# Issuing one 2 MB weight load of a decode kernel as sixteen loads of 8 partitions

## The chip, the cores and the metric

The kernel runs on one core of one Trainium2 chip. The time is that of the device for one execution, in microseconds (us), median of several executions; most executions of one kernel agree within 0.3%. Profiles are single executions, read with times from the start of the span. "Engine" with a number (engine 5) means one of the core's 16 DMA engines; the compute engines are called by name (TensorE, VectorE). SP is the sequencer that issues nearly all loads, in one queue.

HBM is the memory that the loads read, SBUF the core's on-chip memory that they write, in 128 partitions. A port is one of the doors through which DMA engines write SBUF; which partitions lie behind one port is told where it is needed. A packet is one piece of a load, moved by one engine. A semaphore is a counter that can be waited for; a load counts it up as its parts land.

## The reference

A decode step for one token: modulation vectors from `c`, a layer norm, grouped-query attention over a cache of 65,536 positions, then a gated feed-forward block. Cut to what matters here:

```python
D, F = 1024, 3584
Hq, Hkv, Sk, Dh = 32, 4, 65536, 128
mod = silu(c) @ w_mod                                  # 12.6 MB
x = x + ga * attention(h, k_cache, v_cache, wq, wo)    # caches: 134 MB, wq and wo: 8.4 MB each
h = layernorm(x) * (1 + cb) + sb
x = x + gb * ((gelu(h @ w_gate) * (h @ w_up)) @ w_down)  # three weights of 7.3 MB each
```

All of it is bfloat16, and every byte is read once: 185.6 MB.

## The kernel before

Every large load goes into one of ten slots of 16 KB per partition, in a fixed order, from one queue. A load is issued when the slot's former contents have been used. The products with one token are matmuls with the weight as stationary operand, one per 128 x 128 block. The last thirteen loads are four of the gate projection, four of the up projection and five of the down projection:

```python
    def plan_load(src, view_fn):

        s = len(loads) % NSLOT
        nfill[s] += 1
        job = Job(view_fn(slots[s]), (fill[s], 16 * nfill[s]), s)
        job.src = src
        # ... (cut)

    def issue_ready():

        while issued[0] < len(loads):
            j = loads[issued[0]]
            if j.prev is not None:
                if j.prev.freed is None:
                    return
                SP.wait(j.prev.freed)
            sp.dma_start(j.view, j.src).then_inc(j.tok[0], 16)
            issued[0] += 1

        # ... (cut) the down projection; P = 128, UE = 4, NBF = 7
        wd_v = B_w_down.rearrange("(b p e) n -> p b e n", p=P, e=UE)
        while b + 2 < NBF:                     # three loads of 2 MB
            jb = plan_load(
                wd_v[:, b:b + 2, :, :],
                lambda t: t[:, 0:2 * UE * D].rearrange("p (b e n) -> p b e n", b=2, e=UE),
            )
            j_d.append((jb, jb.view.rearrange("p b e n -> p (b e) n"), b * UE, 2 * UE))
            b += 2
        while b < NBF:                         # two loads of 512 KB
            for e in range(0, UE, 2):
                jb = plan_load(wd_v[:, b, e:e + 2, :], flat(2, D))
                j_d.append((jb, jb.view, b * UE + e, 2))
            b += 1

        # ... (cut) the product: waits for one load after the other
            for (jb, view, k0, nk) in jobs:
                PE.wait(jb.tok)
                for kk in range(nk):
                    for j in range(nblk):
                        w = pick(view, kk, j) if pick else view[:, kk, j * P:(j + 1) * P]
                        ins = pe.matmul(bank[:, j:j + 1], w, rhs[:, k0 + kk:k0 + kk + 1], ...)
```

A 2 MB load of the down projection is 16 packets of 8 KB on each of the 16 engines. The third of them, the one that is changed, is called load 90 below (the count is from 0); 88 and 89 are the two before it, 91 and 92 the two of 512 KB behind it.

## Time and profile before

| | before |
|---|---|
| time, median | 455.26 us |
| profiled span | 454.3 us |
| DMA | 409 GB/s from HBM over the span |
| TensorE | 76% busy |

Two rows of the page cut the span into 40 slices of 11.4 us: the mean busy share of the 16 DMA engines in tenths, and what they moved.

```profile
DMA  8999999999999999999999999999999999999972
GB/s 331 429 421 421 430 420 431 418 428 423 421 424 428 423 421 431 421 423 427 423 427 423 426 421 428 423 423 428 418 428 423 426 421 427 413 419 416 419 324 108
```

The engines are busy at about 420 GB/s to the last two slices, so the kernel is bound by its loads. In the last two slices the rate falls to 324 and 108 GB/s. The table of windows shows this closer. Its columns are the stretch in us, its length, busy time and number of instructions of each compute engine, the granted clock of TensorE (as a share of full speed), the mean busy share of the DMA engines and GB/s.

```profile
core 0: us, PE busy (x) PEld busy (x) DVE busy (x) ACT busy (x) POOL busy (x), PEclk, DMA share, GB/s
425.00:430.00 5.00, 2.67 (x80) 2.58 (x78) 0.00 (x0) 0.00 (x0) 0.00 (x0) 0.50 1.02 421
...
435.00:440.00 5.00, 1.96 (x71) 1.91 (x69) 0.18 (x1) 0.00 (x0) 0.00 (x0) 0.50 0.78 323
440.00:445.00 5.00, 1.98 (x75) 1.90 (x73) 0.00 (x0) 0.00 (x0) 0.00 (x0) 0.50 0.51 206
445.00:450.00 5.00, 1.89 (x71) 1.80 (x68) 0.00 (x0) 0.00 (x0) 0.00 (x0) 0.50 0.39 159
```

From 440 us half of the DMA engines have nothing left to do (share 0.51) and the rate is half (206 GB/s). The chain of waits, in order of time, shows that the kernel waits for the other half (start, length, what):

```profile
426.01 24.83 DMA slot<-in_B_w_down_dram
...
450.89 0.60 PE kt_ps L278 x16
...
451.52 0.17 DVE t_dn L532
...
452.35 0.28 DVE y_row L538
```

The issue of the last load begins at 426 us, the load lands at 450.85, and 0.6 us of matmuls and about 3 us of small steps, the store of the result among them, end the kernel. TensorE isn't the limit:

```profile
438.54 1.85 PE L278 MATMUL kt_ps<-u_col,slot 128*128 128x1 bf16 x64 [3.04 <-DMA slot<-in_B_w_down_dram]
...
443.40 1.86 PE L278 MATMUL kt_ps<-u_col,slot 128*128 128x1 bf16 x64 [3.02 <-DMA slot<-in_B_w_down_dram]
...
448.38 2.29 PE L278 MATMUL kt_ps<-u_col,slot 128*128 128x1 bf16 x80 [3.12 <-DMA slot<-in_B_w_down_dram]
...
450.89 0.59 PE L278 MATMUL kt_ps<-u_col,slot 128*128 128x1 bf16 x16 [0.22 <-DMA slot<-in_B_w_down_dram]
```

The first three groups of matmuls wait about 3 us each for their load, the last one 0.22 us (the bracket gives the idle time before it and what ended it).

Every engine adds one to a load's semaphore when its part has landed, so the semaphore records of the trace give sixteen landings per load, in us:

```
load 0   6.50 to 7.55, all sixteen within 1.1 us
load 88  424.90 424.98 425.04 425.61 425.67 425.75 426.97 427.86 | 435.90 435.98 436.11 436.12 436.49 437.18 437.61 438.41
load 90  434.85 434.94 434.98 435.56 435.61 435.69 436.92 437.81 | 445.82 446.02 446.03 446.39 447.10 447.44 447.52 448.34
load 92  437.38 437.46 437.51 438.07 438.12 438.21 439.42 440.30 | 448.35 448.53 448.91 449.61 449.95 450.04 450.26 450.85
```

Eight engines run ahead of the other eight, by 11 us at the end. I call them the early and the late eight. The distance grows slowly over the whole kernel. The page has 61 packets of instruction fetch, about 1.07 us each by their records, whose durations repeat with period eight. If they fall on the late eight, each has 61 x 1.07 / 8 = 8.2 us of them, most of the 11.

### The profile page before, as it was taken

The page shows a single profiled execution, that of the slowest core. Times are in us where ns is not written, and L with a number is a line of the kernel's source. Part 1 is how long each engine was busy: PE and PEld are TensorE (multiplying, and loading weights), DVE is VectorE, ACT ScalarE, POOL GpSimd, SP SyncE. Part 2 cuts the span into 40 slices and gives each one's busy share as a digit, 9 for nine tenths or more (in the row PEclk, how much of TensorE's full clock was granted, in tenths as well). Part 3 has the DMA queues.
Part 4 walks back from the last instruction along what each step waited for, and adds up shares of the span by engine and source line. Part 5 has one row for each costly group of instructions (what it writes and reads, how often), then busy time and mean ns, then how long its engine had stood idle before and what let it go on. Part 6 is the DMA issues. An engine that isn't in the chain of part 4 may idle for free.

```text
span 454.3 us, 16671 instructions
## 1 busy us (share of the span) xinstructions
PE 347.1 (76%) x7849; PEld 336.6 (74%) x7849; DVE 161.7 (36%) x237; ACT 143.2 (32%) x548; POOL 3.7 (1%) x21
## 2 busy tenths in 40 slices
PE   1333478989998999989898998979998985554434
PEld 1333468979988998989898998969987974554434
DVE  1000037444645354444554444544454443110000
ACT  1000013454533335453333354533344534000000
POOL 2000000000000000000000000000000000000000
PEclk9999999785879568776868676895598775555555
DMA  8999999999999999999999999999999999999972
GB/s 331 429 421 421 430 420 431 418 428 423 421 424 428 423 421 431 421 423 427 423 427 423 426 421 428 423 423 428 418 428 423 426 421 427 413 419 416 419 324 108
DMA packets 15428, 186.67 MB, mean 411 GB/s; under 512 B 1536, under 2 KB 1536, under 8 KB 3840
## 3 DMA queue, kind: packets, MB, share of 16 engines
q1 hardware_dynamic: 15328, 185.61, 97.0%
q8 instruction: 61, 1.00, 0.9%
q14 instruction: 7, 0.06, 0.0%
q10 hardware_dynamic: 32, 0.00, 0.0%
HBM read 185.60 MB, written 0.00 MB: 409 GB/s over the span
## 4 chain that ended last, share of the span: by engine, by line
DMA 80%; PE 15%; ACT 2%; SPq 1%; DVE 1%; issue 1%
DMA slot<-in_A_v_cache_dram 59%; DMA slot<-in_A_wq_dram 9%; DMA slot<-in_B_w_up_dram 7%; PE kt_ps L350 6%; DMA slot<-in_B_w_down_dram 5%; PE b L420 4%; PE sc_ps L371 2%; PE kt_ps L278 1%; SPq L182 1%; ACT p_sb L407 1%; PE sc_ps L278 0%; ACT kt_sb L362 0%; PE b L388 0%; PE b L395 0%; DVE Rmat L480 0%
## 5 line engine op out<-in xcount | busy, mean ns | idle before, releaser
L350 PE MATMUL kt_ps<-ident,slot 128*128 128x128 bf16 x2048 | 181.8, 260 | 5.8 <-DMA slot<-in_A_k_cache_dram 3.5
L350 PEld LDWEIGHTS kt_ps<-ident,slot 128*128 128x128 bf16 x2048 | 157.1, 119 | 9.0 <-DMA slot<-in_A_k_cache_dram 3.9
L362 DVE COPY kt_sb<-kt_ps 128x2048 bf16<-128x2048 bf16 x96 | 117.6, 1225 | 106.5 <-PE kt_ps L350 105.6
L362 ACT ACTIVATE kt_sb<-kt_ps 128x2048 bf16<-128x2048 bf16 x32 | 60.1, 1877 | 229.4 <-PE kt_ps L350 229.4
L420 PE MATMUL b<-p_sb,slot 128*128 128x8 bf16 x2048 | 72.3, 168 | 25.6 <-DMA slot<-in_A_v_cache_dram 17.2
L420 PEld LDWEIGHTS b<-p_sb,slot 128*128 128x128 bf16 x2048 | 66.4, 101 | 27.3 <-DMA slot<-in_A_v_cache_dram 18.8
L407 ACT ACTIVATE p_sb<-sc_ps,mneg 128x64 bf16<-128x64 f32 x256 | 83.7, 559 | 4.8 <-DVE mneg L401 4.7
L407 ACT ACTIVATION_READ_ACCUMULATOR p_sb<-sc_ps,mneg 128x1 f32 x256 | 77.2, 362 | 0.0
L371 PE MATMUL sc_ps<-q_col,kt_sb 128*128 128x8 bf16 x2048 | 68.4, 167 | 1.6 <-issue 1.6
L371 PEld LDWEIGHTS sc_ps<-q_col,kt_sb 128*128 128x128 bf16 x2048 | 66.0, 100 | 2.2 <-issue 2.0
L278 PE MATMUL kt_ps<-h_col,slot 128*128 128x1 bf16 x448 | 16.2, 172 | 19.0 <-DMA slot<-in_B_w_up_dram 10.6
L278 PEld LDWEIGHTS kt_ps<-h_col,slot 128*128 128x128 bf16 x448 | 15.6, 118 | 19.7 <-DMA slot<-in_B_w_up_dram 10.9
L390 DVE TENSOR_REDUCE mg<-b 8x1 f32<-8x128 f32 x32 | 8.9, 279 | 41.9 <-PE b L388 41.9
L278 PE MATMUL sc_ps<-s_col,slot 128*128 128x1 bf16 x384 | 11.5, 165 | 15.7 <-DMA slot<-in_w_mod_dram 15.7
L384 DVE TENSOR_REDUCE m_col<-sc_ps 128x8 f32<-128x512 f32 x32 | 21.8, 681 | 4.3 <-PE sc_ps L371 4.3
L278 PEld LDWEIGHTS sc_ps<-s_col,slot 128*128 128x128 bf16 x384 | 11.0, 105 | 16.3 <-DMA slot<-in_w_mod_dram 16.3
L278 PE MATMUL sc_ps<-h_col,slot 128*128 128x1 bf16 x256 | 7.4, 165 | 12.8 <-DMA slot<-in_A_wq_dram 12.8
L278 PEld LDWEIGHTS sc_ps<-h_col,slot 128*128 128x128 bf16 x256 | 7.1, 104 | 13.2 <-DMA slot<-in_A_wq_dram 9.5
L395 PE MATMUL b<-negi,mg 8*128 8x8 f32 x64 | 15.8, 318 | 0.4 <-DVE mg L390 0.4
L395 PEld LDWEIGHTS b<-negi,mg 8*128 8x128 f32 x64 | 12.8, 249 | 2.5 <-DVE mg L390 0.6
L278 PE MATMUL kt_ps<-u_col,slot 128*128 128x1 bf16 x224 | 6.6, 165 | 9.4 <-DMA slot<-in_B_w_down_dram 9.4
L278 PEld LDWEIGHTS kt_ps<-u_col,slot 128*128 128x128 bf16 x224 | 6.3, 104 | 9.7 <-DMA slot<-in_B_w_down_dram 6.6
(71 smaller groups left out, 56.4 us busy)
## 6 DMA issues: line engine op xcount, KB each, us to landing
slot<-in_A_k_cache_dram SPq DMA_DIRECT2D x32, 2048.0 KB, 40.6
slot<-in_A_v_cache_dram SPq DMA_DIRECT2D x32, 2048.0 KB, 44.6
slot<-in_w_mod_dram SPq DMA_DIRECT2D x8, 1536.0 KB, 18.4
slot<-in_A_wq_dram SPq DMA_DIRECT2D x4, 2048.0 KB, 38.3
slot<-in_A_wo_dram SPq DMA_DIRECT2D x4, 2048.0 KB, 43.3
slot<-in_B_w_gate_dram SPq DMA_DIRECT2D x4, 1792.0 KB, 39.4
slot<-in_B_w_up_dram SPq DMA_DIRECT2D x4, 1792.0 KB, 31.2
slot<-in_B_w_down_dram SPq DMA_DIRECT2D x3, 2048.0 KB, 32.2
```

Source lines behind the costliest of these rows:

```text
L182: sp.dma_start(j.view, j.src).then_inc(j.tok[0], 16)
L278: ins = pe.matmul(bank[:, j:j + 1], w, rhs[:, k0 + kk:k0 + kk + 1], start=first, stop=True, skip_group_check=True,)
L350: ins = pe.transpose(kt_ps[:, half * 2048 + t * P:half * 2048 + (t + 1) * P], j_k[i].view[:, b * TB + t, :], ident[:, :],)
L362: ev[(i, b)] = E_.done(act.activation(dst, src, ACT.Copy) if E_ is AC else dve.tensor_copy(dst, src))
L371: ins = pe.matmul(sc_ps[:, base + n * REP:base + (n + 1) * REP], kt_sb[:, i % 2, n, :], q_col[:, g * REP:(g + 1) * REP], start=True, stop= ...
L384: mx[i] = DVE.done(dve.tensor_reduce(m_col[:, i % 2, :].unsqueeze(2), sc_view(i), AX.X, ALU.max))
L390: mx[i] = DVE.done(dve.tensor_reduce(mg8[:, i % 2:i % 2 + 1], b6[0:REP, 32:32 + P], AX.X, ALU.max))
L395: pe.matmul(b6[:, 256:256 + REP], mg8[:, i % 2:i % 2 + 1].to_broadcast([REP, P]), negi[:, :], start=True, stop=True,)
L407: act.activation(p_sb[:, i % 3, :, h], scv[:, h, :], ACT.Exp, bias=mneg[:, i, h:h + 1], scale=scale, accum_out=z_all[:, i, h:h + 1],)
L420: ins = pe.matmul(b7[:, i * REP:(i + 1) * REP], j_v[i].view[:, n, :], p_sb[:, i % 3, n, :], start=(n == 0), stop=(n == CH - 1),)
```

## The change

The intent is to even this out: load 90 is taken from all sixteen engines and given to the eight lowest alone. A load of 8 partitions has only eight shares, and the Trainium skill ("DMA: Bandwidth & Descriptors", section "Why a DMA increments its semaphore by 16 and not by 1") says that such a load runs on the lowest-numbered eight.

```diff
-    def plan_load(src, view_fn):
+    def plan_load(src, view_fn, parts=P):
+
         s = len(loads) % NSLOT
-        nfill[s] += 1
+        nfill[s] += P // parts
         job = Job(view_fn(slots[s]), (fill[s], 16 * nfill[s]), s)
         job.src = src
+        job.parts = parts
@@ issue_ready
-            sp.dma_start(j.view, j.src).then_inc(j.tok[0], 16)
+            n = j.parts
+            for a in range(0, P, n):
+                sp.dma_start(j.view[a:a + n], j.src[a:a + n]).then_inc(j.tok[0], 16)
             issued[0] += 1
@@ the 2 MB loads of the down projection
                 lambda t: t[:, 0:2 * UE * D].rearrange("p (b e n) -> p b e n", b=2, e=UE),
+                8 if b + 4 >= NBF else P,
             )
```

## The prediction

> **What bounds the kernel now.** DMA. The page's rows show the DMA engines 90% busy or more until the last two slices; the chain that ended last is 80% DMA. From 434 us that changes: the window table has DMA share 0.99 at 408 GB/s (434 to 436), then 0.51 at 206 GB/s (440 to 445) and 0.49 at 202 (445 to 448). Half of the engines have finished. The trace's semaphore records show it per load: the third down-projection load lands on eight engines at 434.9 to 437.8 us and on the other eight at 445.8 to 448.3. The last load ends at 440.3 and 450.9. The distance grows from 0.4 us at the first load to 11 us. The late eight also run the 61 instruction fetches (about 1.07 us each by the packet records, rotating with period eight). The two 8-row loads at the start, which run on the lowest eight engines, give packets that follow on engines without fetches. So the late half is engines 8 to 15.
>
> **What the change does.** In the 8 KB packets of the down projection an engine needs 0.312 us each, with 16 or with 8 engines working. The 2 MB load is 16 such packets per engine, 5.0 us. The change takes 5.0 us from each late engine and gives 5.0 us to each early one. If nothing else happened, both halves would end near 445.5: 5 us saved (estimate 450).
>
> **Cost.** The Trainium skill ("SBUF — State Buffer", Door 1: The DMA port swizzle) gives 27.6 GB/s measured for partitions 0 to 3 (one port) and 104 for 0 to 15 (four). Here an engine moves 8 KB in 0.312 us, 26 GB/s, about one port's rate. A load of 128 partitions gives each engine its own port. A load of 8 partitions reaches two, so four engines share one. If the eight engines march through the sixteen loads in step, a packet takes up to four times 0.312 us, and the 2 MB take up to 39 us in place of 9.7. They aren't quite in step: their landings of the load before spread over 3 us, and one engine spends 0.63 us on its partition. I worked out equal sharing of ports with the trace's start times in random engine order (estimate): the early half takes 17 to 25 us for the load from about 430 us and ends 2 to 10 us after 450.9, median 5. The upper 64 partitions also collide with the late engines' own ports.
>
> Issue: a queue instruction took 0.33 us unblocked; sixteen, about 5 to 8 us from 416.9 us, are ready before 430. TensorE follows each load with 0.6 to 1.9 us of matmuls and isn't the limit. All of this lies on the critical path, since the last two loads queue behind the sixteen.
>
> **Prediction.** 459.5 us, range 450 to 468 (8 in 10). Faster by over 2%: 0.01; within 2%: 0.78; slower by over 2%: 0.21.
>
> **Signs.** Down-projection packets of 8 KB on the early eight well above 0.312 us (0.5 to 1.2); late engines done near 445 to 449, early ones last; DMA share about half in the last 10 us as before, at less than 200 GB/s; the chain's down-projection wait longer than 24.8 us. Bytes unchanged; the first 415 us unchanged.
>
> **What would make it wrong.** If ports don't limit here, packets stay at 0.312 us and the time is about 450. If the eight fall fully into step, it is above 470. If the issuing queue blocks on full rings, engines 8 to 15 could run dry before the last two loads.

## The result, and the profile after

(Here and below, the time of before is that of the runs beside the kernel in question.)

| | before | after |
|---|---|---|
| time, median | 455.48 us | 470.93 us |
| range | 455.22 to 455.77 | 470.53 to 471.12 |
| ratio | 1 | 1.0338, 95% interval 1.0320 to 1.0356 |
| profiled span | 454.3 us | 469.3 us |
| HBM read | 185.60 MB | 185.60 MB |

Ratios here and below are the mean time of one kernel's fast runs over that of the other's fast runs of the same rounds, so not quite the ratio of the medians. The change costs 15.4 us, nearly four times what I forecast, and lies outside the range.

The same rows and windows of the page of the changed kernel:

```profile
DMA  8999999999999999999999999999999999999950
GB/s 342 427 420 422 429 422 429 423 420 428 427 422 423 423 427 422 427 425 423 422 428 425 423 423 427 425 423 425 426 421 423 426 424 414 417 419 344 221 147 29
```

```profile
425.00:430.00 5.00, 2.66 (x81) 2.58 (x78) 0.00 (x0) 0.00 (x0) 0.00 (x0) 0.50 1.02 413
430.00:435.00 5.00, 0.68 (x21) 0.60 (x19) 0.00 (x0) 0.00 (x0) 0.00 (x0) 0.50 0.90 216
435.00:440.00 5.00, 1.88 (x56) 1.80 (x54) 0.18 (x1) 0.00 (x0) 0.00 (x0) 0.50 0.95 221
440.00:445.00 5.00, 1.12 (x42) 1.15 (x43) 0.00 (x0) 0.00 (x0) 0.00 (x0) 0.50 0.96 221
445.00:450.00 5.00, 0.73 (x28) 0.64 (x25) 0.00 (x0) 0.00 (x0) 0.00 (x0) 0.50 0.87 174
450.00:455.00 5.00, 1.86 (x64) 1.78 (x64) 0.00 (x0) 0.00 (x0) 0.00 (x0) 0.50 0.59 175
455.00:460.00 5.00, 0.00 (x0) 0.00 (x0) 0.00 (x0) 0.00 (x0) 0.00 (x0) 0.50 0.14 51
460.00:465.00 5.00, 1.61 (x60) 1.62 (x61) 0.00 (x0) 0.00 (x0) 0.00 (x0) 0.50 0.10 43
```

Two things are new. From 430 to 445 us nearly all engines are busy (0.90 to 0.96), but at 216 to 221 GB/s, half of the former rate. From 455 us on, a tenth of the engines is busy (0.10 of 16 engines is 1.6), and these run on for 11 us.

```profile
slot<-in_B_w_down_dram SPq DMA_DIRECT2D x2, 2048.0 KB, 42.0
slot<-in_B_w_down_dram SPq DMA_DIRECT2D x16, 128.0 KB
```

The sixteen loads of 128 KB are there (the last column, the time to landing, is given only for the ordinary ones). In the chain the wait for the last load goes from 24.83 to 29.21 us, and it begins 10.6 us later:

```profile
434.85 1.80 PE kt_ps L283 x50
436.65 29.21 DMA slot<-in_B_w_down_dram
...
465.90 0.60 PE kt_ps L283 x16
```

(The page's own chain of this kernel puts 83% down to "issue". The semaphore of the sixteen loads also has one record at each issue, by the same section of the skill for the eight engines that aren't used, and I take it that the inference of releasers loses its way there. The end of the chain, above, is sound.)

TensorE waits for each load as before, only longer:

```profile
443.88 1.85 PE L283 MATMUL kt_ps<-u_col,slot 128*128 128x1 bf16 x64 [7.00 <-DMA slot<-in_B_w_down_dram]
...
452.11 1.86 PE L283 MATMUL kt_ps<-u_col,slot 128*128 128x1 bf16 x64 [6.38 <-DMA slot<-in_B_w_down_dram]
...
463.39 2.29 PE L283 MATMUL kt_ps<-u_col,slot 128*128 128x1 bf16 x80 [9.41 <-DMA slot<-in_B_w_down_dram]
```

The packet records say more. Packets of 8 KB took 0.31 us until about 429 us, in both kernels. In the changed kernel those that start between 436 and 446 us took 0.54 to 0.60 us in the median of each 2 us, and that is true of the late eight too: their parts of load 88 landed at 439.5 to 443.8 us instead of 435.9 to 438.4, those of load 89 at 448.9 to 452.1 instead of 440.9 to 443.4. After 454 us, packets of 0.31 us again, but only as many as two engines can have. In the semaphore records of load 92 fourteen landings come by 456.8 us, and two at 463.9 and 465.9.

### The profile page after: what moved, and what is told of

It is laid out like the page before. It is cut to its first block, busy times and chain, and to the rows that moved or that the text cites. A ratio compares the mean times of both kernels' runs of the same rounds, so it can differ in the third digit from the quotient of the medians.

```text
span 469.3 us, 16686 instructions
## 1 busy us (share of the span) xinstructions
PE 344.0 (73%) x7849; PEld 333.6 (71%) x7849; DVE 161.7 (34%) x237; ACT 143.1 (30%) x548; POOL 3.7 (1%) x21
## 3 DMA queue, kind: packets, MB, share of 16 engines
HBM read 185.60 MB, written 0.00 MB: 396 GB/s over the span
## 4 chain that ended last, share of the span: by engine, by line
issue 83%; DMA 14%; PE 1%; DVE 0%; POOLq 0%; ACTq 0%; POOL 0%; ACT 0%; DVEq 0%
DMA slot<-in_B_w_up_dram 7%; DMA slot<-in_B_w_down_dram 6%; DMA x_row<-in_A_x_dram 1%; PE kt_ps L283 1%; PE b L308 0%; POOLq L549 0%; ACTq L197 0%; POOL rs L318 0%; PE b L541 0%; DVE hn L320 0%; DVE y_row L543 0%; ACT th_col L266 0%; DVE ht L327 0%; DVE y_col L539 0%; DVE t_dn L537 0%
## 5 line engine op out<-in xcount | busy, mean ns | idle before, releaser
L355 PE MATMUL kt_ps<-ident,slot 128*128 128x128 bf16 x2048 | 179.5, 258 | 6.7 <-DMA slot<-in_A_k_cache_dram 3.7
L355 PEld LDWEIGHTS kt_ps<-ident,slot 128*128 128x128 bf16 x2048 | 154.8, 118 | 8.8 <-DMA slot<-in_A_k_cache_dram 4.7
L283 PE MATMUL sc_ps<-s_col,slot 128*128 128x1 bf16 x384 | 11.5, 166 | 15.9 <-DMA slot<-in_w_mod_dram 15.9
L400 PE MATMUL b<-negi,mg 8*128 8x8 f32 x64 | 15.4, 311 | 0.4 <-DVE mg L395 0.4
```

Source lines behind the costliest of these rows:

```text
L355: ins = pe.transpose(kt_ps[:, half * 2048 + t * P:half * 2048 + (t + 1) * P], j_k[i].view[:, b * TB + t, :], ident[:, :],)
L400: pe.matmul(b6[:, 256:256 + REP], mg8[:, i % 2:i % 2 + 1].to_broadcast([REP, P]), negi[:, :], start=True, stop=True,)
```

## The experiments

The first round sets four theories against each other. Theory P: several engines crowd on one write port of SBUF (the destination). Theory S: neighbouring rows of HBM are read at once (the source). Theory O: a fixed cost of sixteen small loads. Theory G, a form of P: one crowded port holds up everybody. Runs timed in rounds and their profiles were in the fast state; the three kernels with tiny loads and the one without arithmetic ran once, so their state is unknown, and their times are only told.

**Spread on both sides.** Each of the sixteen loads takes 8 partitions 4 apart instead of 8 neighbours. The Trainium skill ("DMA: Bandwidth & Descriptors", "The descriptor swizzle") has loads of all 128 partitions served so that engine 0 gets partitions 0 to 3 and 32 to 35, engine 1 the next four of each, engines 8 to 15 the upper 64 partitions in the same way, each engine writing a port of its own. With a spacing of 4, and if the eight shares go to the eight lowest engines in order, each of them writes its own port for the lower 64 partitions, and that of the engine numbered 8 higher for the upper 64.

```diff
-                sp.dma_start(j.view[a:a + n], j.src[a:a + n]).then_inc(j.tok[0], 16)
+                w = slice(a, a + n) if n == P else slice(a // 32 * 32 + a % 32 // 8, a // 32 * 32 + 32, 4)
+                sp.dma_start(j.view[w], j.src[w]).then_inc(j.tok[0], 16)
```

> Same sixteen loads of 8 partitions, but each takes partitions 4 apart (p, p+4, ..., p+28), on both sides, result still correct. Theory P (four engines crowd on one SBUF write port): the crowding of four goes away; the first eight loads run near 0.312 us per 8 KB packet, the last eight share each port with one late engine; 450 to 457 us, so within 1% of before. Theory S (HBM: eight neighbouring 8 KB rows read at once are slow): also gone here, 450 us. Theory O (a fixed cost of sixteen small loads: issue, semaphores, ring): stays near 471 us.

Measured: correct, 466.0 us, ratio 1.0232 (1.0215 to 1.0250). No theory had this: 4.8 us better than the change, but 10.6 us worse than before. The windows show why the number lies between:

```profile
430.00:435.00 5.00, 2.37 (x67) 2.20 (x64) 0.18 (x1) 0.00 (x0) 0.00 (x0) 0.50 0.89 367
435.00:440.00 5.00, 0.08 (x4) 0.11 (x5) 0.00 (x0) 0.00 (x0) 0.00 (x0) 0.50 1.03 226
440.00:445.00 5.00, 1.76 (x64) 1.68 (x63) 0.00 (x0) 0.00 (x0) 0.00 (x0) 0.50 0.87 183
...
455.00:460.00 5.00, 2.01 (x75) 2.02 (x76) 0.00 (x0) 0.00 (x0) 0.00 (x0) 0.50 0.10 43
```

While the lower 64 partitions are written (430 to 435 us) the rate is nearly full; all packets of 8 KB started before 434 us took 0.31 us. While the upper 64 are written (435 to 445 us), packets take 0.61 to 0.62 us in the median of each 2 us from 436 to 444 us, with none below 0.59 us from 438 to 444, on all the engines that are still busy: sixteen at first, fourteen (0.87 of 16) after 440 us. And again a tenth of the engines runs on from 455 us at full speed. The semaphore records settle how many: 96 of the 128 landings of the sixteen loads come by 449.8 us, 16 for each of six engines; the other 32 form two even rows of 16, one every 0.62 us, which begin after 446 us and end at 456.6 and 457.9.

**Destination and source apart.** Two kernels with a wrong result.

```diff
 # ... (cut) w as in the run before; then, first kernel
+                sp.dma_start(j.view[a:a + n], j.src[w]).then_inc(j.tok[0], 16)
 # second kernel
+                sp.dma_start(j.view[w], j.src[a:a + n]).then_inc(j.tok[0], 16)
```

> Wrong result on purpose: each of the sixteen loads reads rows 4 apart as in the run before it, but writes 8 neighbouring partitions as the change does. Theory P (destination): near 471 us, all engines' packets at 0.5 to 0.6 us. Theory S (source): near 450 us. Theory O: 471 us.

> Wrong result on purpose: each load reads 8 neighbouring rows as the change does, but writes partitions 4 apart. Theory P: 450 to 457 us, as the run with both sides spread. Theory S: near 471 us. Theory O: 471 us.

Measured: neighbours in SBUF and spread rows in HBM 470.3 us (ratio 1.0325); neighbours in HBM and spread partitions in SBUF 466.05 us (1.0232). The two numbers are those of the change and of the kernel before this one. The destination makes the difference and the source none: theory S falls.

**The lower half only.** Eight loads of 8 neighbours for partitions 0 to 63, and one ordinary load for 64 to 127.

```diff
 # ... (cut) the count of the semaphore: 9 loads instead of 16
-            for a in range(0, P, n):
+            for a in range(0, P, n) if n == P else range(0, P // 2, n):
                 sp.dma_start(j.view[a:a + n], j.src[a:a + n]).then_inc(j.tok[0], 16)
+            if n != P:
+                sp.dma_start(j.view[P // 2:], j.src[P // 2:]).then_inc(j.tok[0], 16)
```

> Only partitions 0 to 63 go as eight loads of 8 neighbouring partitions; partitions 64 to 127 as one load, which has all 16 engines. Theory P with separate ports: while the eight small loads run, the late engines write other ports and keep 0.27 to 0.31 us per packet, the early ones are slowed to 0.5 us and more; about 455 to 460 us. Theory P with a common path in front of the ports: the late engines are slowed to 0.5 us or more too, as in the changed kernel, for about half as long; 460 to 465 us.

Measured: correct, 467.8 us (ratio 1.0271), worse than either forecast. All of the late eight were slowed: their parts of load 88 landed at 440.3 to 445.9 us, against 435.9 to 438.4 before, and packets took about 0.6 us in the median from 430 to 442 us. That speaks for a common path, but the run is not clean, for two reasons that I hadn't thought of. The load of 64 partitions shares ports itself (0.53 us in the median at 448 to 450 us). And, as the next experiment shows, two of the early engines are not among the eight lowest; they came to that load at about 430 us, so the upper ports weren't free of foreign writers. The kernel without arithmetic below decides it.

**Who is early?** Behind the last load of the kernel before, sixteen tiny loads of 1 to 16 rows, each on a semaphore of its own. If a load of k rows runs on the k lowest engines, each load adds one engine to those of the load before it, and the landings name the engines.

```diff
 # ... (cut) the semaphores and their waits; this comes once the last load is issued
+            for k in range(1, 17):
+                sp.dma_start(mark[0:k, (k - 1) * 32:k * 32],
+                    A_x[0, 0, 0:k * 32].rearrange("(p c) -> p c", c=32)).then_inc(msem[k - 1], 16)
```

> The kernel before with sixteen tiny loads (1 to 16 rows of 64 bytes, each on its own semaphore) behind the last load. A load of k rows uses the k lowest engines, so the landings tell which of the engines end early (near 440 us) and which late (near 450 us). If the eight lowest are all early, as I predicted, the load of 8 rows lands eight times near 440 us. The records of the run with both sides spread say otherwise: 96 of its 128 landings come before 448.2 us and two engines start after 446 us; so I now expect six early and two late among the eight lowest. Time as before, 455 to 457 us.

Measured: 455.66 us, correct. Every load of k rows has exactly k landings (and, below 16, one record at its issue). The landing of each engine in the first tiny load that uses it:

```
engine   0      1      2      3      4      5      6      7      8      9      10     11     12     13     14     15
us     438.3  440.3  437.7  439.8  438.6  448.8  449.8  437.5  437.7  450.6  450.1  450.3  450.3  448.5  449.0  438.2
```

The early eight are 0 to 4, 7, 8 and 15. The late eight are 5, 6 and 9 to 14. So two of the eight engines that the change loads with more work are late ones. (The counts agree with the skill's rule for the choice of engines.)

The same tiny loads behind the last load of the spread kernel and of the change:

> The same sixteen tiny loads behind the last load of the kernel with both sides spread: 466 to 468 us. Two of the eight lowest engines end near 459 to 461 us, the other six near 448 to 452; the two early engines that are not among the lowest eight end near 441 us.

> The changed kernel with the sixteen tiny loads behind the last one: engines 5 and 6 end last, near 463 and 466 us, all others by 457 us; 471 to 472 us in all.

Measured: 466.3 and 470.7 us, both correct.

```
engine             0      1      2      3      4      5      6      7
spread, us       448.9  451.4  448.7  450.1  449.3  459.1  461.3  448.8
the change, us   453.3  456.8  452.0  455.3  453.0  464.0  465.7  451.8
```

In both, engines 5 and 6 end 7 to 10 us after the last of the other six, and load 92 has landed on all engines but two by 451.8 and 456.6 us. Engines 5 and 6 are what the kernel waits for at the end.

**Ports alone.** A kernel without arithmetic (a wrong result), in stages with a wait between them. Each stage issues small loads with 4 packets of 8 KB per partition, and behind them four ordinary loads, so that the engines outside the small loads work beside them.

```python
        stage("base", [], 4)
        stage("own", own(0, 4) * 3, 4)          # 8 partitions, 4 apart, in 0 to 31
        stage("other", own(1, 4) * 3, 4)        # the same in 64 to 95
        stage("adj", [slice(8 * a, 8 * a + 8) for a in range(4)] * 3, 4)
        stage("otheralone", own(1, 4) * 3, 0)   # no ordinary loads beside
        stage("adjalone", [slice(8 * a, 8 * a + 8) for a in range(4)] * 3, 0)
        stage("four", [slice(0, 4)] * 3 + [slice(32, 36)] * 3, 4)
        stage("fouralone", [slice(0, 4)] * 3 + [slice(32, 36)] * 3, 0)
        # ... (cut) one, oneown, two
```

> Wrong result on purpose: no arithmetic, only loads, in stages with a wait between them. Each stage issues small loads (4 packets of 8 KB per partition) and behind them four ordinary loads of 128 partitions, so that the engines outside the small loads work beside them. base: ordinary loads alone, 0.312 us per packet. own: 8 partitions 4 apart in 0 to 31. other: the same in 64 to 95. adj: 8 neighbours. four: 4 neighbours. one and two: one or two engines, into partitions 68 to 71. Theory P with independent ports (an engine shares only the port it writes to): other: two writers per port, 0.6 us; adj alone: up to 1.2 us for the small loads; four alone 1.2 us; one: only that engine and one other at 0.6 us, all others at 0.312. Theory G (one crowded port holds up everybody): in one, two, adj and other all sixteen engines are slowed to about 0.6 us while the small loads last. own should run at 0.312 us in both.

Measured, in windows inside the stages base, own, other, adj, otheralone, adjalone, four and fouralone, in this order (there was no compute, so the columns are length, POOL, granted clock, DMA share, GB/s):

```profile
27.00:35.00 8.00, 0.00 (x0) 1.00 1.01 426
56.00:59.00 3.00, 0.00 (x0) 1.00 1.01 421
94.00:102.00 8.00, 0.00 (x0) 1.00 1.03 213
133.00:169.00 36.00, 0.00 (x0) 1.00 1.02 142
197.00:207.00 10.00, 0.00 (x0) 1.00 0.50 208
214.00:254.00 40.00, 0.00 (x0) 1.00 0.51 67
265.00:285.00 20.00, 0.00 (x0) 1.00 1.01 105
314.00:336.00 22.00, 0.00 (x0) 1.00 0.25 27
```

Read the last two columns. Four engines that write the same four partitions move 27 GB/s together (share 0.25, last line). That agrees with the Trainium skill ("SBUF — State Buffer", "Door 1: The DMA port swizzle"), which measured 27.6 GB/s for partitions 0 to 3. With the twelve other engines working beside them on their own ports, all sixteen are busy (1.01) at 105 GB/s in all: every packet, also those of engines that share no port with anybody, took 1.25 us, four times 0.31. Eight engines in 64 to 95 run at full rate alone (208 GB/s on half of the engines); with the owners of these ports beside them, all sixteen run at half rate (213 GB/s). In that stage every one of the sixteen shares a port with another, so it doesn't set P and G apart. Small loads as such cost nothing: in the stage own the rate is that of the stage base while they last (second line). So theory O falls. Theory P in its independent form falls by the stage four, and theory G holds there: one port with four writers held up everybody. Whether ports with two writers do so too is settled by the control in the last experiment (`BASE = 64`), where only eight engines share.

Two stages didn't do what I meant. A load of one partition with four runs ran on four engines, not on one, so one was another case of four writers on one port beside the port's owner: all sixteen engines at about 1.53 us (oneown, four writers with the owner among them: 1.25 us). And in two, with two partitions per load, three engines took about 1 us per packet and the others 0.39 us: held up, but by a quarter and not by a factor of three. How strongly the rest is held up in mixed cases stays open.

**The two late engines alone.** What does the extra work of engines 5 and 6 cost when no port is shared? The spread kernel, with the upper 64 partitions' rows written to scratch in the partitions that each engine serves anyway (a wrong result).

```diff
 # ... (cut) w as in the spread kernel
+                dst = j.view[w]
+                if n != P and a >= 64:
+                    dst = kt_sb[w.start - 64:w.stop - 64:4, 0, :, :]   # ... (cut) 16 KB per partition, free by then
-                sp.dma_start(j.view[w], j.src[w]).then_inc(j.tok[0], 16)
+                sp.dma_start(dst, j.src[w]).then_inc(j.tok[0], 16)
```

> Wrong result on purpose: the sixteen loads of the kernel with both sides spread, but the last eight write scratch in partitions 0 to 31 and 32 to 63, so that each of the eight lowest engines writes only the partitions that it serves anyway. Bytes, engines and issues as there. What is left is the second load on the two late engines 5 and 6: sixteen packets, 5.0 us. They end at 448.6 and 449.6 us before, so the last landing moves from 450.5 to 454.6: 459 to 460 us, all packets at 0.312 us. If sharing ports is not what slows the packets, it stays at 466 us.

Measured: 460.0 us, ratio 1.0087 (1.0071 to 1.0102), 4.0 us over before, as forecast. From 435 to 440 us the DMA engines move 396 GB/s where the spread kernel has 226 (the line above), and packets of 8 KB took 0.31 us in the median from 430 to 450 us:

```profile
435.00:440.00 5.00, 1.85 (x64) 1.79 (x64) 0.18 (x1) 0.00 (x0) 0.00 (x0) 0.50 0.96 396
440.00:445.00 5.00, 1.87 (x64) 1.79 (x64) 0.00 (x0) 0.00 (x0) 0.00 (x0) 0.50 0.62 247
445.00:450.00 5.00, 0.00 (x0) 0.00 (x0) 0.00 (x0) 0.00 (x0) 0.00 (x0) 0.50 0.14 56
450.00:455.00 5.00, 2.46 (x86) 2.38 (x87) 0.00 (x0) 0.00 (x0) 0.00 (x0) 0.50 0.09 36
```

Load 92 lands on fourteen engines by 445.3 us, 5.6 us before the last one of before: this is the gain that the change was after. It lands on the other two at 453.4 and 454.8.

**A shift that keeps to the findings.** The engines to be loaded are the lowest four (all early), and they may write only the partitions that they serve anyway. Then the data has to lie in these partitions: the last 512 rows of `w_down` go 16 to a partition into partitions 0 to 15 and 32 to 47, by loads of 4 partitions 4 apart. Eight small matmuls with columns of the identity move the matching values of u there. The product with these rows uses partitions 0 to 47, with zeros in u for 16 to 31.

```diff
+        wl = B_w_down[(NBF - 1) * UE * P:NBF * UE * P, :].rearrange("(q t) n -> q t n", t=16)
+        pieces = [
+            (slice(BASE + 32 * h + r, BASE + 32 * h + 16, 4), slice(16 * h + r, 16 * h + 16, 4))
+            for h in range(2) for r in range(4)
+        ]                                       # BASE = 0; destination and source partitions
+        for t in (0, 8):
+            jb = plan_load(wl[:, t:t + 8, :], flat(8, D), pieces)
 # ... (cut) the rest of the loads behind these, the move of u, and the product
```

> A different way to shift work, on the kernel before: the last 512 rows of the down projection (1 MB) are laid 16 to a partition into partitions 0 to 15 and 32 to 47, by loads of 4 partitions 4 apart, which run on engines 0 to 3 alone, each into the partitions that it serves in ordinary loads too. u of these rows is moved there by eight small matmuls. The loads of the rest follow. If the time is set by which engines carry the bytes and no foreign port is written, the twelve other engines are spared 64 KB each, 2.5 us at 0.312 us per 8 KB, and engines 0 to 3 get 7.5 us more and end by 448 us: 452.5 to 454 us. If small loads on few engines slow everybody in any case, it is above 456 us.

Measured: correct, 455.67 us, ratio 1.0001 (0.9988 to 1.0013), so the time missed its forecast. The loads did what was forecast: the last landing is at 448.66 us (before: 450.85), and packets of 8 KB stay at 0.31 us in the median. But the chain now ends differently:

```profile
406.84 36.80 DMA slot<-in_B_w_down_dram
...
443.69 7.30 PE kt_ps L290 x256
...
451.01 0.18 DVE t_dn L560
```

TensorE works 7.30 us without a pause: it took the small loads' weights after those of load 89, for which it had waited until 443.64 us, and the gain of 2.2 us became a backlog of TensorE.

The control has one number changed, `BASE = 64`: the rows go to partitions 64 to 79 and 96 to 111, which engines 8 to 11 serve.

> The same kernel with one number changed: the rows go to partitions 64 to 79 and 96 to 111, which engines 8 to 11 serve in ordinary loads. Same engines, loads, bytes and matmuls. If a shared port holds up all engines, packets of all engines go to about 0.6 us for as long as the small loads last (20 us), and the time is 460 to 465 us. If ports were independent, only engines 8 to 11 would lose time, up to 10 us on three of the late engines: also up to 463 us, but with the packets of engines 5, 6, 12 to 14 at 0.312 us. If the destination doesn't matter, as own4.

Measured: correct, 467.2 us, ratio 1.0263 (1.0248 to 1.0279), 11.5 us above its twin by the medians, and 2 us above what I had given. Between 432 and 448 us the packets of 8 KB took 0.64 to 0.66 us in the median of each 2 us, and none less than 0.56 us. Here only engines 0 to 3 and the owners 8 to 11 share a port, two to each, so the others at work were held up as well. The last landing came at 460.0 us. One window of each, first the twin:

```profile
435.00:440.00 5.00, 2.30 (x79) 2.13 (x77) 0.51 (x3) 0.00 (x0) 0.00 (x0) 0.50 0.80 328
```

```profile
435.00:440.00 5.00, 2.29 (x64) 2.11 (x64) 0.53 (x3) 0.00 (x0) 0.00 (x0) 0.50 1.03 205
```

Bytes, engines, loads and the number of matmuls are the same, and the destination makes 328 or 205 GB/s.

At last, TensorE's order mended in the first of the two: the weights of the first small-load group are used between those of loads 88 and 89, when TensorE was idle.

```diff
-        matvec(acc_bank["dn"], j_d, u_col, (v_uc,), KD)
-        matvec(acc_bank["dn"], j_l, u_l, (v_l,), KD, first=False, rows=slice(BASE, BASE + 48))
+        matvec(acc_bank["dn"], j_d[:1], u_col, (v_uc,), KD)
+        matvec(acc_bank["dn"], j_l[:1], u_l, (v_l,), KD, first=False, rows=lo)
+        matvec(acc_bank["dn"], j_d[1:], u_col, (v_uc,), KD, first=False)
+        matvec(acc_bank["dn"], j_l[1:], u_l, (v_l,), KD, first=False, rows=lo)
 # ... (cut) lo = slice(BASE, BASE + 48); the last loads' product follows as before
```

> own4 with one change on TensorE only: the weights of the first small-load group, which landed at 438.3 us in own4 while TensorE sat idle from 440.6 to 443.7, are used before those of the second 2 MB load. In own4 the last byte landed at 448.7 us, 2.2 us earlier than before, and TensorE then ran 3 us behind. With 1.9 us taken off that backlog: 453.5 to 454.5 us, 0.3 to 0.5% faster than before. If it isn't TensorE that ate the gain, 455.5 us again.

Measured: correct, 454.01 us, as forecast, ratio 0.9967 (0.9954 to 0.9979). It beats both kernels, by 0.33% over the one before, clear of noise.

```profile
443.46 3.56 PE kt_ps L290 x124
...
447.35 2.07 PE kt_ps L290 x68
...
449.45 0.18 DVE t_dn L563
```

TensorE's last matmuls end 1.6 us earlier than in the run before.

## Why the prediction was wrong

**Where the time went.** By the ratios, times 455.5 us: the extra work on engines 5 and 6 costs 4.0 us (ownonly). Sharing the ports of the upper 64 partitions costs 6.6 more (spread, 10.6 in all). Writing 8 neighbours instead of 8 partitions 4 apart costs 4.8 more (the change, 15.4). The three were taken off one after the other; in another order the shares could differ.

The prediction had two terms: 450 us if ports don't limit, and 9.5 us more for crowded ports. The runs show 460.0 us without shared ports, and 10.9 us more with them. So nearly all of the miss of 11.4 us is in the first term, the engines. That the second came out near is in part luck, since the sum behind it slowed only the engines that share a port.

**Point by point.**

- "DMA", with half of the engines done 11 us early: right. The chain and the windows showed it, and shifting bytes to four early engines did move the last landing.
- "So the late half is engines 8 to 15": wrong, and this is the step that failed. The late eight are 5, 6 and 9 to 14. I inferred it from records that followed the two 8-row loads at the start: six of the eight engines with such packets had no fetch, and two seemed to have one, which I took for a mix-up in following the packets. Engines 5 and 6 are the two late ones among the eight lowest. The change therefore takes 5.0 us from six late engines only and gives 5.0 us to two of them, which end the kernel. The estimate of 5 us saved couldn't have come about even on free ports: the kernel with free ports is 4.0 us slower than before (460.0 us, not 450).
- "A load of 8 partitions reaches two [ports], so four engines share one": right in kind; four engines on one port move 27 GB/s together.
- "Equal sharing of ports", with only the sharers slowed: wrong. The whole set of engines was slowed. The signs had the late engines done near 445 to 449 us and the early ones last. In the run with the tiny loads behind the change, the late engines 9 to 14 had their parts of load 92 between 452.7 and 455.2 us (the landings that are left when those of the other ten are taken out), and two late engines, 5 and 6, came last of all.
- "The early half takes 17 to 25 us for the load from about 430 us": about right. In the run with the tiny loads, engines 0 to 4 and 7 ended at 451.8 to 456.8 us, 2.5 us of which are the two loads behind.
- "Ready before 430": wrong, without effect. The sixteen issues lasted from 416.8 to 434.8 us and the last load's to 441.4. Engines 8 and 15 ran dry meanwhile, which cost nothing at the end: engines 5 and 6 had work until 464 us and more.
- Signs: packets above 0.5 us, bytes unchanged, the first 415 us unchanged, the wait in the chain longer than 24.8 us (29.2): right. DMA share of a half in the last 10 us: wrong, 0.10 to 0.14, two engines.

**What stays open.** Why a crowded port holds up engines that don't write it. The Trainium skill ("DMA: Bandwidth & Descriptors", "Back-pressure in remote DMA") tells of a saturated destination port that clogs the path back to the engines that share it, for transfers between cores; the runs here show the like for loads from HBM, but not the mechanism. No run changed the instruction fetches, so that they make the late eight late isn't shown by experiment. The landings in the trace of the kernel before speak for it. Add up by how much the eight late landings of a load come behind its first one: from one load to the next (loads 8 to 92) this sum grew by 1.55 us in the median where one fetch began between (59 times), and by 0.06 us where none did (25 times). The same sum for the early eight grew by 0.01 us in the median in both cases. By this estimate a fetch costs its engine 1.55 us and not the 1.07 us of its record, and 61 x 1.55 / 8 = 11.8 us is the whole distance.

## What to carry to other kernels

Before work is moved to "idle" DMA engines, name them: tiny loads of 1 to 16 rows behind the last load cost 16 issues and tell which engine ends when. A load that is confined to few engines must also keep to the partitions that these engines serve in ordinary loads; otherwise it slowed all sixteen here, whoever carried the bytes: by a quarter for the engines outside the crowd in the mildest case (the stage two), fivefold in the worst (the stage one). And when the loads' end does move, look at once what TensorE was still doing then: the first version of the better shift lost all of its 2.2 us to an order of matmuls that had never mattered.

## What the Trainium skill lacked or had wrong

- "SBUF — State Buffer" gives the rate of a crowded port, and the runs agree (27 GB/s for four engines on partitions 0 to 3). That such a port holds up other engines stands in "DMA: Bandwidth & Descriptors" for transfers between cores alone ("Back-pressure in remote DMA"), without a number; for loads from HBM no page has it: all sixteen at 1.25 us per 8 KB packet instead of 0.31, 105 GB/s in all, while twelve of them wrote ports of their own.
- "SBUF — State Buffer" says that port numbers aren't engine numbers, but nowhere is it a rule for authors that a load on fewer than 16 engines should write the partitions that these engines serve in full loads. One number decided 455.67 or 467.2 us in two kernels otherwise alike.
- "DMA: Bandwidth & Descriptors", "Latency and other measured facts", has engines 7 and 15 as usually slower and ties that, as a best guess, to loads issued from GpSimd. In these loads, issued from SP, both are early, and engines 5, 6 and 9 to 14 end 10 to 13 us after them, in a kernel with 61 instruction fetches of about 1.07 us by their records. No page that I read says on which engines instruction fetches run.
